# Order of the phi(k) loads on GpSimd and of the first w_down sums in a fused forward and backward kernel

## The chip, the cores and the metric

The kernel runs on one core of a Trainium2 chip. The metric is the device time of one execution in microseconds (us). Before the change it is 802.19 us, the median of 3 runs (800.33 to 802.31).

## The reference

A block of linear attention and a SwiGLU block, both behind a layer norm, forward and backward, with 2048 tokens, model width 640, 32 heads of 20, and an inner width of 1728. Inputs and outputs are bfloat16.

```python
phi = lambda t: where(t > 0, t + 1, exp(t)) + 1e-6
q, k, v = split(layernorm(x) @ wqkv)            # 32 heads
kv = einsum("hsd,hse->hde", phi(k), v);  z = phi(k).sum(over s)
o  = (phi(q) @ kv) / (phi(q) @ z + 1e-6)        # per head
h  = x + o @ wo
g, u = silu(layernorm(h) @ w_gate), layernorm(h) @ w_up
out = h + (g * u) @ w_down
# outputs: out, and the gradients of x, wqkv, wo, w_gate, w_up, w_down for a given grad_out
```

Here m = g * u, dm is its gradient, and dk, dq, dwqkv and so on are gradients. Two things of it matter below: the gradient of k needs phi(k) again late in the kernel, and `(g * u) @ w_down` is computed last of all.

## The kernel before, in words

The 2048 tokens are 16 tiles of 128 (`ST`), the width 640 is 5 blocks of 128 (`DT`), and the inner width is 4 groups of 448, 448, 448 and 384 (`GW`). TensorE (PE) multiplies into PSUM, of which a ring of 4 tiles of two banks is used. VectorE (DVE) and ScalarE (ACT) read them out. DMAs are issued from the queues of SyncE (SP), GpSimd (POOL) and ACT; each queue issues in order, so an issue that waits holds back the ones behind it. What is needed again much later is stored in scratch tensors in device memory: phi(k) in `scr_pk`, m in `scr_m`, the transposed gradients of gate and up in `scr_dT`, h in `scr_h1`.

The kernel is written with a scheduler. Inside `with tc.manual_schedule(engines={...})` the named engines keep the order of the program; the other engines' instructions are placed by the scheduler, which may put one far ahead of the place where it is written, if its operands and buffers allow it. `pool_store` (L162) issues a DMA from POOL through `keep_in_program_order`, so that it is not placed ahead; `pool_load` (L159) and a plain `nc.gpsimd.dma_start` do not.

The stages, in order, with their place in the profiled span of 803.4 us:

1. Layer norm, q, k and phi, kv, attention, and h (to about 160 us).
2. For each of the 4 groups of the inner width: gate and up, SwiGLU and its gradient (L731 to L772), and then the three weight gradients (`dw_group`, L627 to L706). The gradients of gate and up go through a transposing DMA into a `stg` tile (tag `stg`, 3 buffers) and from there to `scr_dT`. In `dw_group`, the blocks of the gradient of w_down and one row block of the others are plain products over 16 tiles (`dw`, L797 to L812); the other four row blocks are done with 7 products in place of 8, on sums and differences that DVE makes (`tt`, L642; `prod`, L646). Results are copied to `dwev` tiles of the ring `f` (6 buffers, shared with `s1` and with the SwiGLU stage) and stored from POOL (L652, L810). The end of `dw_group` in group 3 is: product with T4, `ev = fw("dwev")` filled from `pc` and `u3` by DVE, then the last product into `pc` (`ps_wc`), which has to wait until DVE has read `pc`. Group 3 ends at about 444 us.
3. The gradient of h through gate and up (`ps_dhn`, with `cols` tiles of two token tiles loaded from `scr_dT`: 0 and 1 from ACT's queue, the rest from POOL's), the gradient through wo (`ps_dp`), and dq, per token tile; to about 600 us.
4. The gradient of k and of x. Step t of the loop over 16 + 3 steps makes dk of tile t from `ps_dk` and phi(k) (`load_pk` loads tile t + 2, L933; `pkr` uses the `stg` buffers too; DVE reads it at L1037 and L1043) and dx of tile t - 3 (`ps_dxn`, then `ln_bwd`), which POOL stores (L1077). Blocks of dwqk (`dwqk_steps`, L981 to L993) stand between. SP and DVE keep program order, POOL does not.
5. The last stage, from about 730 us: out = h + m @ w_down, two token tiles a pair. Pairs 0 to 6 are done with 7 products per pair in place of 8: DVE makes T1 to T5 from w_down once and four sums S1 to S4 of m for each pair (`osum(p, i)` makes S(i+1) of pair p). PE takes `step_a` (two products of which DVE reads both, L1157 to L1163), `step_b` (S1 and T1), `step_c` (S2 and T2, into a bank that `step_a` used), `step_d` (S3, T3), `step_e` (T4, T5) and `step_f` (S4). Steps d to f of a pair run inside the next pair's turn. The last two token tiles are plain products (`tail`). Between them stand small blocks: dW_o in 6 blocks (`dwo`), dW_v in 5 (`dwv`), and what is left of dwqk (`fill`). PE and ACT keep program order here, DVE, SP and POOL are scheduled.

The change touches `load_pk` (L931 to L933), the list `small_q` (L1135) and the order of the last stage (L1202 to L1290).

Of the kernel before, what the change touches and what calls it, by code (L numbers as in the profile page):

```python
# [20 lines left out]
def kernel(  # L21
# [8 lines left out]
    nc = tc.nc  # L30
# [4 lines left out]
    DT = D // P  # L35
# [26 lines left out]
    def mm(name):  # L62

        return psum.tile([P, 2, 512], FP32, name=name, tag="mm")

    def row(ps):
        return ps[:, :, :320]

    def half(ap):
        return ap.rearrange("p (c n) -> p c n", c=2)  # L70
# [3 lines left out]
    def wk(name, w=D, pool=0):  # L74
        return wpools[pool].tile([P, w], BF16, name=name, tag="w", padded_shape=[P, D])

    def dram_tm(name, W):
        t = dram.tile([S, W], BF16, name=name)
        return t, t.rearrange("(t p) w -> p t w", p=P)

    scr_xnT = dram.tile([ST, P, DT, P], BF16, name="scr_xnT")
    scr_pk, scr_pk_v = dram_tm("scr_pk", D)
# [31 lines left out]
    HG = len(OH)  # L114
# [47 lines left out]
    def pool_store(out, in_):  # L162
        tc.keep_in_program_order(nc.gpsimd.dma_start(out=out, in_=in_))
# [452 lines left out]
    with tc.manual_schedule(engines={EngineType.SP}):  # L616
# [105 lines left out]
        for g in range(4):  # L722
# [4 lines left out]
            for t in range(0, ST, 2):  # L727
# [11 lines left out]
                tt = t % 8  # L739
# [183 lines left out]
    with tc.manual_schedule(engines={EngineType.SP, EngineType.DVE}):  # L923
# [5 lines left out]
        pkrs = {}  # L929

        def load_pk(t):  # L931
            pkrs[t] = small.tile([P, D], BF16, name="pkr", tag="stg", bufs=3, padded_shape=[P, 7 * P])
            nc.gpsimd.dma_start(out=pkrs[t][:], in_=scr_pk_v[:, t, :])  # L933

        load_pk(0)
        load_pk(1)
        def tr_cols(dst, src, c):
# [141 lines left out]
        def dwo(j):  # L1079
            h0, h1 = HC[j]  # L1080
            ev = wk("dwo", pool=j % 2)
            ps = mm("ps_dwo")
            for ci, (n0, n1) in enumerate(NCH):
                nc.tensor.matmul(ps[:, ci, :320], lhsT=KV[:, j, :], rhs=G[:, j, n0:n1], start=True, stop=True)
            nc.scalar.copy(out=half(ev[:]), in_=row(ps))
            nc.gpsimd.dma_start(out=out_3[OH[j] + h0:OH[j] + h1, :], in_=ev[h0:h1, :])
# [10 lines left out]
        def load_h1(t):  # L1097
            h1rs[t] = wk("h1r", pool=t % 2)
            nc.gpsimd.dma_start(out=h1rs[t][:], in_=scr_h1_v[:, t, :])
# [6 lines left out]
        B21, B22 = wd[:, HK:2 * HK, 0:320], wd[:, HK:2 * HK, 320:D]  # L1106
        T1, T2, T3, T4 = (ot[:, i * HK * 320:(i + 1) * HK * 320].rearrange("p (k n) -> p k n", k=HK) for i in range(4))
        T5 = ot[:, 4 * HK * 320:4 * HK * 320 + D].rearrange("p (k n) -> p k n", k=2)
# [5 lines left out]
        def os_v(p, i):  # L1114
            o = (4 * (p % 2) + i) * HK * P
            return os[:, o:o + HK * P].rearrange("p (k c) -> p k c", c=P)

        def mblk(p, r, k):
            t = 2 * p + r
            return mTs[t // 4][:, t % 4, k * HK:(k + 1) * HK, :]  # L1120

        def tt(out, in0, in1, op=ALU.subtract):
            nc.vector.tensor_tensor(out=out, in0=in0, in1=in1, op=op)

        def osum(p, i):

            if p < NP:
                S1, S2, S3, S4 = (os_v(p, k) for k in range(4))
                a11, a12, a21, a22 = mblk(p, 0, 0), mblk(p, 0, 1), mblk(p, 1, 0), mblk(p, 1, 1)
                (lambda: tt(S1, a21, a22, ALU.add), lambda: tt(S2, S1, a11), lambda: tt(S3, a11, a21),  # L1130
                 lambda: tt(S4, a12, S2))[i]()

        pa = {}
        pcc = None
        small_q = [(dwv, i) for i in range(DT)]  # L1135

        def prod(out, lhs, rhs, start, stop):
            for k in range(HK):
                nc.tensor.matmul(out, lhsT=lhs[:, k, :], rhs=rhs[:, k, :], start=(start and k == 0),  # L1139
                                 stop=(stop and k == HK - 1), skip_group_check=not start)  # L1140
# [8 lines left out]
        BL = (wd[:, 12:14, 0:320], wd[:, 12:14, 320:D])  # L1149

        def h1v(t, ci):
            return h1rs[t][:, 320 * ci:320 * ci + 320]

        def bank(p):
            return pa[p][:, 0, :320], pa[p][:, 1, :320], pcc[:, p % 2, :320]
# [13 lines left out]
        def step_c(p):  # L1169
            A = bank(p)[0]  # L1170
            prod(A, os_v(p, 1), T2, False, True)
            tt(u2h[p % 2], A, h1v(2 * p, 1), ALU.add)

        def step_d(p):
            A = bank(p)[0]
            left(A, 2 * p + 1, BL[1], 1, which=(1, 0))
            prod(A, os_v(p, 2), T3, False, True)
            tt(u3h, A, h1v(2 * p + 1, 1), ALU.add)
# [24 lines left out]
        with tc.manual_schedule(engines={EngineType.PE, EngineType.Activation}):  # L1203
            for t in range(4):
                load_h1(t)
            for t in (5, 6):
                load_mT(t)
            for j in range(2):
                tr_cols(Y[:, j, :], scr_Yt, OH[j])
            tt(T1, B12, B11)  # L1210
            osum(0, 0)
            tt(T2, B22, T1)
            osum(0, 1)
            tt(T3, B22, B12)
            osum(0, 2)
            tt(T4, B21, T2)
            tt(T5, BL[0], BL[1])
            osum(0, 3)
            fill = dwqk_steps(1, 3)
            for j in range(4):  # L1220
                next(fill)
                dwo(j)
            fill = dwqk_steps(1, 4)
            next(fill)
            dwo(4)
            pcc = mm("ps_oc")

            for p in range(NP):
                v = p - 1
                load_h1(2 * p + 4) if 2 * p + 4 < ST else None  # L1230
                load_h1(2 * p + 5) if 2 * p + 5 < ST else None
                for t in (2 * p + 7, 2 * p + 8):
                    if t < ST:
                        load_mT(t)
                for j in range(2 * p + 2, min(2 * p + 4, HG)):
                    tr_cols(Y[:, j, :], scr_Yt, OH[j])
                step_a(p)
                if v < 0:
                    next(fill)
                    osum(p + 1, 0)  # L1240
                    step_b(p)
                    step_c(p)
                    next(fill)
                    osum(p + 1, 2)
                    next(fill)
                    osum(p + 1, 1)
                    dwo(5)
                    osum(p + 1, 3)
                    continue
                step_d(v)  # L1250
                step_b(p)
                c22(v)
                osum(p + 1, 0)
                step_c(p)
                step_e(v)
                osum(p + 1, 2)
                step_f(v)
                osum(p + 1, 1)
                osum(p + 1, 3)
                if p >= 3:  # L1260
                    f, i = small_q.pop(0)
                    f(i)

            pso = {}

            def tail(u, n0, n1, out):
                for j in range(FT - 1):
                    nc.tensor.matmul(out, lhsT=mTs[u // 4][:, u % 4, j, :], rhs=wd[:, j, n0:n1],
                                     start=(u == ST - 2 and j == 0), stop=(u == ST - 1 and j == FT - 2))

            v = NP - 1
            p14 = mm("ps_o")
            tail(ST - 2, 0, 320, p14[:, 0, :320])
            step_d(v)
            tail(ST - 2, 320, D, p14[:, 1, :320])
            c22(v)
            step_e(v)
            step_f(v)
            p15 = [mm("ps_o") for _ in range(2)]
            o15 = [p15[ci % 2][:, ci // 2, :n1 - n0] for ci, (n0, n1) in enumerate(CH15)]  # L1280
            parts = [(ST - 2, n0, n1, p14[:, ci, :320]) for ci, (n0, n1) in enumerate(NCH)]
            parts += [(ST - 1, n0, n1, o15[ci]) for ci, (n0, n1) in enumerate(CH15)]
            for n, (u, n0, n1, out) in enumerate(parts):
                r = slice(64 * (n % 2), 64 * (n % 2) + 64)
                nc.tensor.matmul(out, lhsT=mTs[u // 4][r, u % 4, FT - 1, :], rhs=wd[r, FT - 1, n0:n1],
                                 start=(u == ST - 1), stop=(u == ST - 2))
            tt(half(h1rs[ST - 2][:]), row(p14), half(h1rs[ST - 2][:]), ALU.add)
            o_store(ST - 2)
            for f, i in small_q:
                f(i)  # L1290
            h1r = h1rs.pop(ST - 1)
            for ci, (n0, n1) in enumerate(CH15):
                tail(ST - 1, n0, n1, o15[ci])
                tt(h1r[:, n0:n1], o15[ci], h1r[:, n0:n1], ALU.add)
                (nc.sync, nc.scalar, nc.sync)[ci].dma_start(out=o0_v[:, ST - 1, n0:n1], in_=h1r[:, n0:n1])
# [30 lines left out]
```

## Time and profile before

| what | value |
|---|---|
| median of 3 runs | 802.19 us (800.33 to 802.31) |
| the profiled execution's own time | 805.1 us |
| its span, first to last instruction | 803.4 us |
| mean granted clock of PE in it | 0.996 of full speed |
| PE busy | 792.6 us, 99% |
| DVE, ACT, POOL busy | 566.8, 287.8, 172.6 us |
| DMA, mean over the span | 199 GB/s |

The profile is of one execution, in microseconds from the first instruction. A row of a timeline has a start, a length, the engine, the line, the operation, what is written and read, and how many instructions were merged; in brackets stands how long the engine had been idle and what released it. A view of waits has the engine and line that waited, what it waited for, the total, how often, and the longest. The rows of "stretches" have the stretch, its length, the busy time and count of PE, of its weight loads (PEld), of DVE, ACT and POOL, then the granted clock, the DMA share and GB/s. Matmuls are pipelined and their ends are modelled, so that the start of the next one says more than the end of a row.

### The profile page before, as it was taken

To read this page: it belongs to the slowest core of one execution; us is meant where nothing else is said; L and a number is where in the kernel's file an instruction comes from. 1 tells how busy PE (TensorE), PEld (TensorE's weight loads), DVE (VectorE), ACT (ScalarE), POOL (GpSimd) and SP (SyncE) were. 2 spreads that over 40 slices of the span, in tenths; PEclk is the share of its full clock that TensorE was granted. 3 is DMA by queue.
4 is the path that set the end of the run, shared out by engine and by line. 5 is a ranking of instruction groups with operands and counts; after the bars stand their busy time and mean duration, and the time that the engine had idled before them with its cause. 6 is when DMAs were issued, how large, how long until landed. Compare 5 with 4: busy or idle time off the path is not lost.

```text
span 803.4 us, 13640 instructions
## 1 busy us (share of the span) xinstructions
PE 792.6 (99%) x5315; PEld 506.5 (63%) x5315; DVE 566.8 (71%) x1015; ACT 287.8 (36%) x414; POOL 172.6 (21%) x305
## 2 busy tenths in 40 slices
PE   9999999999999999999997999999999999999998
PEld 7676566555555555555664677777777777776665
DVE  7979988894496658844954158999897366535673
ACT  7963532750382146303811123223313133323010
POOL 4600047311201110112133101111221121113320
PEclk9999999999999999999998999999999999999999
DMA  9899999999589967992897647877499869999992
GB/s 257 169 242 314 183 232 253 255 287 228 129 187 242 214 158 197 220 217 63 193 231 156 253 119 204 222 200 166 117 245 175 157 133 155 182 233 264 244 196 81
DMA packets 286706, 160.11 MB, mean 199 GB/s; under 512 B 241565, under 2 KB 275486, under 8 KB 286641
## 3 DMA queue, kind: packets, MB, share of 16 engines
q1 hardware_dynamic: 268912, 99.56, 61.5%
q0 software_dynamic: 14832, 54.36, 22.0%
q10 hardware_dynamic: 2896, 5.33, 2.2%
q8 instruction: 41, 0.67, 0.4%
q14 instruction: 25, 0.20, 0.1%
HBM read 47.68 MB, written 53.66 MB: 126 GB/s over the span
## 4 chain that ended last, share of the span: by engine, by line
PE 87%; DVE 4%; DMA 4%; issue 2%; SPq 1%; POOL 0%; ACT 0%; DVEq 0%; POOLq 0%; ACTq 0%
PE ps_dhn L108 15%; PE ps_dxn L1069 8%; PE ps_dw L806 8%; PE ps_wa L646 6%; PE pu L736 6%; PE pg L731 6%; PE ps_dm L417 5%; PE ps_dwqk L986 5%; PE ps_kq L305 4%; PE ps_oa L1139 3%; PE ps_wc L646 3%; PE ps_dp L108 3%; PE ps_y L508 3%; PE ps_gt L861 3%; PE ps_dk L108 3%; PE ps_a L571 3%
## 5 line engine op out<-in xcount | busy, mean ns | idle before, releaser
L108 PE MATMUL ps_dhn<-wgT,cols 128*128 128x320 bf16 x864 | 119.5, 299 | 0.0
L108 PEld LDWEIGHTS <-cols 128*128 128x128 bf16 x864 | 84.6, 98 | 33.0 <-issue 0.2
L146 DVE CUSTOM_DVE_ANT_0 lb_a<-lb_dy,hn 128x640 bf16<-128x640 bf16 x32 | 26.4, 825 | 59.0 <-ACT lb_dy L144 59.0
L736 PE MATMUL pu<-wgu,hnT 128*128 128x448 bf16 (+1 forms) x320 | 63.6, 346 | 0.0
L731 PE MATMUL pg<-wgu,hnT 128*128 128x448 bf16 (+1 forms) x320 | 63.6, 346 | 0.0
L806 PE MATMUL ps_dw<-m_s,dh 128*128 128x448 bf16 (+1 forms) x320 | 60.4, 346 | 0.0
L1069 PEld LDWEIGHTS <-ring 128*128 128x128 bf16 x480 | 47.0, 98 | 18.2
L1069 PE MATMUL ps_dxn<-wqkvT,ring 128*128 128x320 bf16 x320 | 51.3, 299 | 0.0
L736 PEld LDWEIGHTS <-hnT 128*128 128x128 bf16 x320 | 31.3, 98 | 27.1
L806 PEld LDWEIGHTS <-dh 128*128 128x128 bf16 x320 | 31.3, 98 | 27.1
L731 PEld LDWEIGHTS <-hnT 128*128 128x128 bf16 x320 | 31.3, 98 | 27.0
L417 PEld LDWEIGHTS <-dh2T 128*128 128x128 bf16 x320 | 31.0, 98 | 25.1
L417 PE MATMUL ps_dm<-wdT,dh2T 128*128 128x448 bf16 (+1 forms) x240 | 46.5, 344 | 0.0
L144 ACT ACTIVATE lb_dy<-ps_dhn,rstd 128x640 bf16<-128x640 f32 x16 | 12.7, 793 | 93.8 <-PE ps_dhn L108 93.8
L305 PE MATMUL ps_kq<-wqk,xnT 128*128 128x320 bf16 x320 | 44.9, 299 | 0.4 <-DMA xnT<-xn 0.4
L646 PEld LDWEIGHTS <-S 128*128 128x128 bf16 x256 | 25.7, 101 | 27.8 <-issue 7.1
L752 ACT ACTIVATE dd<-pg 128x896 bf16<-128x896 f32 (+1 forms) x32 | 28.5, 890 | 40.4 <-PE pg L731 38.0
L305 PEld LDWEIGHTS <-xnT 128*128 128x128 bf16 x320 | 30.9, 98 | 12.9 <-DMA xnT<-xn 0.8
L986 PEld LDWEIGHTS <-hn 128*128 128x128 bf16 x320 | 31.0, 98 | 12.0
L772 POOL DMA_DIRECT2D scr_m<-m_s x16 | 12.1, 756 | 122.6 <-DVE m_s L764 122.6
L642 DVE TENSOR_TENSOR dd<-dd 128x3584 bf16<-128x3584 bf16 (+1 forms) x12 | 23.1, 1953 | 21.2 <-PE ps_wa L646 21.2
L150 ACT ACTIVATE lb_a<-hn,lb_k 128x640 bf16<-128x640 bf16 x32 | 29.5, 920 | 21.7 <-DVE lb_k L149 18.8
(210 smaller groups left out, 1528.0 us busy)
## 6 DMA issues: line engine op xcount, KB each, us to landing
scr_dT<-stg SPq DMA_DIRECT2D x48, 224.0 KB, 2.6
cols<-scr_dT POOLq DMA_DIRECT2D x6, 1728.0 KB, 8.3
scr_m<-m_s POOLq DMA_DIRECT2D x12, 448.0 KB, 4.8
cols<-scr_dT ACTq DMA_DIRECT2D x2, 1728.0 KB, 12.0
scr_dT<-stg SPq DMA_DIRECT2D x16, 192.0 KB, 2.3
scr_pq<-pqa SPq DMA_DIRECT2D x4, 640.0 KB, 4.7
scr_xnT<-xnT SPq DMA_DIRECT2D x4, 640.0 KB, 5.2
scr_pk<-pk SPq DMA_DIRECT2D x4, 640.0 KB, 4.5
```

The lines of the kernel that those rows point to most:

```text
L108: nc.tensor.matmul(ps[:, ci, :320], lhsT=lhs(k), rhs=rhs(k, *NCH[ci]), start=(start and k == 0), stop=(stop and k == n - 1))
L146: nc.vector.tensor_tensor_reduce(out=a[:], in0=dy[:], in1=xhat, scale=1.0, scalar=0.0, op0=ALU.mult, op1=ALU.add, accum_out=sums[:, 1:2])
L150: nc.scalar.activation(out=a[:], in_=xhat, func=ACT.Identity, scale=k[:, 1:2], bias=k[:, 0:1])
L305: nc.tensor.matmul(ps[:, ci, :320], lhsT=xnT[:, t, k, :], rhs=wqk[:, k, w0 + n0:w0 + n1], start=(k == 0), stop=(k == DT - 1))
L417: nc.tensor.matmul(ps[:, c, :w], lhsT=dh2T[:, kt, (t + c) * P:(t + c + 1) * P], rhs=wdT[:, kt, o:o + w], start=(kt == 0), stop=(kt == DT - 1))
L646: nc.tensor.matmul(out, lhsT=lhs[:, t, :], rhs=rhs[:, t, :], start=(first and t == 0), stop=(t == 7), skip_group_check=not first)
L731: nc.tensor.matmul(pg[:, c, :w], lhsT=hnT[:, kt, (t + c) * P:(t + c + 1) * P], rhs=wg[:, kt, 0:w], start=(kt == 0), stop=(kt == DT - 1))
L736: nc.tensor.matmul(pu[:, c, :w], lhsT=hnT[:, kt, (t + c) * P:(t + c + 1) * P], rhs=wg[:, kt, w:2 * w], start=(kt == 0), stop=(kt == DT - 1))
L752: sig = nc.scalar.activation(out=dg, in_=pg[:, :, :w], func=ACT.Sigmoid)
L806: nc.tensor.matmul(ps[:, c, :w], lhsT=lhs(t), rhs=rhs(t), start=(t == 0), stop=(t == ST - 1))
L986: nc.tensor.matmul(ps[:, ci, :320], lhsT=xn_r[:, t, i * P:(i + 1) * P], rhs=dq[t // 8][:, t % 8, n0:n1] if which == 0 else dk[:, t, n0:n1] ...
L1069: nc.tensor.matmul(ps[:, ci, :320], lhsT=lhs[:, i, :], rhs=rhs[:, i, n0:n1], start=(k == 0 and i == 0), stop=(k == 2 and i == DT - 1))
```

## The change

Three things are changed, and no instruction is added or removed.

- `load_pk` issues through `pool_store`, so POOL keeps it in program order.
- In the last stage, T4, T5 and S4 of pair 0 (`osum(0, 3)`) are written after `step_a(0)`; S1 and S2 of pair 1 are written after `step_c(0)`, and T5, S4 of pair 0, S3 and S4 of pair 1 at the end of pair 0's turn.
- `dwo(5)` leaves pair 0's turn and becomes the first of `small_q`; one block is taken from it after every pair but 0 and 2 (before: from pair 3 on). The last `dwv` moves from before the last tail to behind the first block of the first tail.

```diff
         def load_pk(t):
             pkrs[t] = small.tile([P, D], BF16, name="pkr", tag="stg", bufs=3, padded_shape=[P, 7 * P])
-            nc.gpsimd.dma_start(out=pkrs[t][:], in_=scr_pk_v[:, t, :])
+            pool_store(pkrs[t][:], scr_pk_v[:, t, :])
...
-        small_q = [(dwv, i) for i in range(DT)]
+        small_q = [(dwo, HG - 1)] + [(dwv, i) for i in range(DT)]
...
             osum(0, 2)
-            tt(T4, B21, T2)
-            tt(T5, BL[0], BL[1])
-            osum(0, 3)
             fill = dwqk_steps(1, 3)
...
                 step_a(p)
                 if v < 0:
+                    tt(T4, B21, T2)
                     next(fill)
-                    osum(p + 1, 0)
                     step_b(p)
                     step_c(p)
+                    osum(p + 1, 0)
+                    osum(p + 1, 1)
                     next(fill)
-                    osum(p + 1, 2)
                     next(fill)
-                    osum(p + 1, 1)
-                    dwo(5)
-                    osum(p + 1, 3)
+                    tt(T5, BL[0], BL[1])
+                    for k, i in ((0, 3), (1, 2), (1, 3)):
+                        osum(p + k, i)
                     continue
...
-                if p >= 3:
+                if p != 2:
                     f, i = small_q.pop(0)
                     f(i)
...
             tail(ST - 2, 0, 320, p14[:, 0, :320])
+            for f, i in small_q:
+                f(i)
             step_d(v)
...
             o_store(ST - 2)
-            for f, i in small_q:
-                f(i)
             h1r = h1rs.pop(ST - 1)
```

With this, the built kernels differ in the order of the instructions as follows. POOL: before, loads 0, 1 and 2 of phi(k) stand between the first two and the next two stores of group 3's `dw` blocks; after, loads 0 and 1 stand behind the last load of x in stage 3 and the others in the step where they are written. DVE: in the last stage the two reads of `step_a(0)` stand ahead of T4, T5 and S4 of pair 0. PE: the two matmuls of `dwo(5)` and the seven of the last `dwv` stand at their new places.

## The prediction

> **What bounds the kernel now.** I read the page first, parts 1 and 2: which engine is full, and at which clock.
>
> ```profile
> PE 792.6 (99%) x5315; PEld 506.5 (63%) x5315; DVE 566.8 (71%) x1015; ACT 287.8 (36%) x414; POOL 172.6 (21%) x305
> ...
> PEclk9999999999999999999998999999999999999999
> ```
>
> TensorE (PE) is busy for 792.6 of 803.4 us. No step of this change removes a matmul, so it can only win idle PE time, 10.8 us in all, and matmuls that ran at a lower clock: slice 22 of 40 (422 to 442 us, the digit 8) is the only one under 9. Next, the waits of PE:
>
> ```profile
> PE ps_wc L646 <- DVE dwev L642: 4.4, 1, 4.4
> ...
> PE ps_oa L1139 <- DVE h1r L1123: 0.7, 1, 0.7
> PE ps_oa L1139 <- ACT dwqk L991: 0.6, 1, 0.6
> ...
> PE ps_dwv L127 <- DVE h1r L1123: 0.2, 1, 0.2
> ```
>
> These four are in code that the change touches, 5.9 us together; the others (1.1, 0.5, 0.4) are at the start. For the large one, the timeline of all engines:
>
> ```profile
> 411.31 0.80 ACT L808 CAST dwev<-ps_dw 128x768 bf16<-128x768 f32 x1 [9.12 <-PE ps_dw L806]
> ...
> 430.72 0.54 POOL L933 DMA_DIRECT2D pkr<-scr_pk  x1 [19.20 <-DMA scr_dT<-stg]
> ...
> 431.91 2.76 PE L646 MATMUL ps_wa<-m_s,hn 128*128 128x384 bf16 x16
> ...
> 434.75 0.54 POOL L933 DMA_DIRECT2D pkr<-scr_pk  x1 [1.74 <-DMA scr_dT<-stg]
> 435.29 1.08 POOL L810 DMA_DIRECT2D out_dram<-dwev  x2
> ...
> 438.10 0.96 DVE L642 TENSOR_TENSOR dwev<-ps_wc,m_s 128x768 bf16<-128x768 f32 x1 [7.37 <-DMA out_dram<-dwev]
> 439.11 5.18 PE L646 MATMUL ps_wc<-dd,S 128*128 128x384 bf16 x16 [4.44 <-DVE dwev L642]
> ...
> 444.13 6.14 PE L108 MATMUL ps_dhn<-wgT,cols 128*128 128x320 bf16 x44
> ```
>
> Three loads of phi(k), which the program writes much later, stand in POOL's queue inside group 3 of the weight gradients. They take `stg` buffers, so they wait for the stores of the last transposed tiles (until 434.1). Behind them stand two stores of a `dwev` buffer that ScalarE had filled by 412.11. They go out at 435.29 and land at 437.98. The next `dwev` of the ring needs that buffer, so VectorE waits 7.37 us and PE 4.44. The clock pays again, in the stretches before and after:
>
> ```profile
> 439.10:444.10 5.00, 4.99 (x16) 2.31 (x16) 0.00 (x0) 0.86 (x2) 2.13 (x4) 0.50 0.82 255
> 444.10:449.10 5.00, 5.00 (x38) 3.60 (x37) 0.96 (x1) 0.00 (x0) 2.36 (x4) 1.00 1.02 396
> ```
>
> The last columns but two are the granted clock: 0.50 for the 16 matmuls after the wait, then 1.00.
>
> **Part 1: loads of phi(k) in program order.** In the changed instruction order they are gone from group 3; loads 0 and 1 follow the last load of x, load t+2 stands in step t. The price of the old place is read from starts. Blocks of 32 matmuls of this shape start at 400.71, 405.91 and 411.11: 5.20 per 32, 2.60 per 16. The block of 431.91 is therefore over at 434.51, and without a wait the last block takes 2.60 more: ps_dhn starts at 437.11 and not at 444.13. That is **7.02 us**: 4.6 of waiting and 2.4 of half clock.
>
> [...] This trace had 5.0 us at 0.50. [...]
>
> What is late next here? (a) The freed stores. They can go out at 412.2, but in the built kernel a POOL transfer also waits for the one issued eight earlier, here a padding store of L163 (the second was issued at 406.94; these land 4.1 to 9.8 us after issue), so the second store goes at 416.7 at the latest. The trace has no such store in this stretch. The nearest rows for its landing: stores of L810 take 1.9 to 13.1 us, the store of `stg` issued at 409.81 beside the load of `cols` took 14.67. I take 13.1, the nearest in time: 429.8; with 14.67, 431.4. VectorE can use the buffer from 432.59, when ScalarE's copy of `u3` ends (432.11 + 0.48), and finishes at 433.6, 0.9 before PE asks. So by every row the term is 7.02, and it can't be more, since PE has no gap left; each us of landing beyond some 17 costs one. (b) `cols` 1 is loaded from ScalarE's queue behind a copy that moves from 439.15 to 434.9: issue about 435.4, landing 9.4 to 14.5 (the two loads of that queue), so 449.9 at worst. It is needed two ps_dhn steps (7.33 each in the chain) after 437.11, at 451.8. Covered by 1.9; before by 5. A later landing by x stalls PE by x - 1.9. (c) `cols` 2, now first to wait for the stores of `stg`, is needed after 466.
>
> GpSimd's issues keep 0.75 us (L772, 752 to 759 ns) while VectorE is busy 3.97 of 4.00 us. [...]
>
> In their new place the loads lie in the dk/dxn loop (one step each 5.44 us). Two of them before the xnT_r loads push those back by 1.07 (583.64 to 584.7, needed at 621.5). Load 2 goes behind the third dwqk store, at 622.7, and lands 2.5 to 6.4 us later, 629.1 at worst; VectorE wants it at 626.03, but its next operation waits for PE until 630.13. Loads 4 and 5 go behind dwqk stores at 630.3 and 636.0; they are read at 643.88 and 649.27. From load 6 on each stands behind dx(t-6): issue 644.8 against a read at 654.72, 9.9 us for a landing of 6.4 at most. Cost 0; bounds 0 and, as a rival, below.
>
> **Part 2: the first pair of w_down.** PE's timeline:
>
> ```profile
> 740.16 0.98 PE L1139 MATMUL ps_oc<-ot,os 128*128 128x320 bf16 x6
> 741.86 0.97 PE L1139 MATMUL ps_oa<-ot,os 128*128 128x320 bf16 x6 [0.72 <-DVE h1r L1123]
> 742.67 2.34 PE L986 MATMUL ps_dwqk<-dk,hn 128*128 128x320 bf16 x16
> 744.85 0.43 PE L1084 MATMUL ps_dwo<-mats 128*128 128x320 bf16 x2
> 745.84 1.79 PE L1139 MATMUL ps_oa<-wd,mT 128*128 128x320 bf16 x12 [0.55 <-ACT dwqk L991]
> ```
>
> A 320-column matmul takes 0.136 (739.07 to 740.16 for 8). Six from 740.16 end at 740.98; the next start is 741.86: **0.88** for the wait on step_a's two reads. VectorE has T4 (1.15), T5 (0.48) and S4 (0.55) ahead of them; now they follow S3, which ends at 738.95, and PE's `left` (739.14), and end at about 740.2. T4 to S4(1), 0.55 each after T4, then end near 745.7, before the next reads can start (746.0). Nothing of PE wants one earlier.
>
> With dwo(5) moved, its PSUM tile is not taken between; the next step_a gets that of dwo(4), copied by 737.86, and no longer waits for the dwqk copy. dwo(5) ends at 744.85 + 0.27 = 745.12, step_a starts at 745.84: **0.72**. dwo(5) itself (0.27 of PE, a copy of 0.70, an issue of 0.54) comes back after pair 1, where the dwv blocks of pairs 3 to 6 show no wait. Its store stands before the load of h1 tile 11, two pairs ahead of its use.
>
> The last dwv took the tile that VectorE freed at 796.47; moved up behind the first tail block it takes one copied at 789.57 before a start at 790.5, and its store leaves SP's queue ahead of three others. **0.15**; its 0.3 of matmuls is only moved. Less cover: SP transposes mT without a pause from 718 to 768, on full DMA engines. The tightest tile is 11: issue 759.15, landing 4.5 to 10.5, 769.7 at worst; VectorE's read moves from 771.45 to 769.85.
>
> **Sum.** 7.02 + 0.88 + 0.72 + 0.15 = 8.77. The profiled execution took 805.1, its span 803.4 and 1.7 around it; less 8.8, 796.3. The median of the runs, 802.19, is 2.9 below it; a wait that hangs on DMA landings may be shorter there by as much. I carry the difference over: 802.19 - 8.77 = **793.4**.
>
> **Rivals.**
> 1. Another wait takes the place in part: `cols` 1, or the freed stores, late. For: DMA is full from 400 to 424, and the cover of `cols` 1 falls to 1.9. Against: all rows end inside it. A stall of 3 us leaves a gain of 5.8 or, with the clock halved again, about 4: 796.4 to 798.2.
> 2. The large wait does not go: another load is hoisted or the store waits otherwise. Only 1.75 remains: 800.4. Against: the new order shows none there.
> 3. Slower: phi(k) arrives late in the loop. The load now stands behind dx, so it has 9.9 us from issue to read. From there each us over it costs VectorE one in each of some 10 steps, and PE after its PSUM tiles are full. A landing of 12 costs 21: 802.2 - 8.8 + 21 = 814. For: POOL transfers of up to 13.1 us exist (410, beside `cols`). Against: 6.4 at most in this loop. It decides for slower from about 10.8.
>
> **How the numbers follow.** Forecast 0.80 (own range 791.5 to 796), rival 1 0.11, rival 2 0.04, rival 3 0.05. The range reaches down by the 2 us that two runs of before differ by, up over the shorter wait (796.3) and into rival 1: 791.3 to 797.5. A measurement tells 0.3%, 2.4 us, from no change. Faster: forecast and rival 1, 0.91; same: rival 2, 0.04; slower 0.05.
>
> **What would show it.** In the changed profile: no wait of ps_wc; out_dram stores of L810 near 412 to 417; ps_dhn some 7 us earlier, at clock 1.00; the second PE wait gone, step_c right behind step_b; no wait on the dwqk copy; pkr reads without idle before them. A wait on `cols` at the third ps_dhn step is rival 1; idle before L1037 is rival 3. I am wrong if the stores of group 3 land after 433.6, or if the clock fell for another reason than the gap.

## The result and the profile after

The changed kernel takes 796.55 us (median of 6 runs, 796.16 to 798.27), the kernel before 801.35 in the same comparison (6 runs, 800.08 to 802.31): a ratio of 0.9945, 95% interval 0.993 to 0.996, 4.8 us less. The forecast was 793.4 with a range of 791.3 to 797.5: direction and range held, the gain was 4.8 and not 8.8. The time lies above the forecast's own range (791.5 to 796) and inside the one given for rival 1 (796.4 to 798.2), though the stall of rival 1 did not occur. The profiled execution of the changed kernel took 796.25 with a span of 794.5; that of before took 805.1 with 803.4. So between the two *profiles* lie 8.9 us, nearly what was forecast for them, and between the *medians* only 4.8. Where the other four went is the question of the experiments.

Page of the changed kernel, parts 1 and 2:

```profile
PE 790.2 (99%) x5315; PEld 506.5 (64%) x5315; DVE 566.9 (71%) x1015; ACT 288.1 (36%) x414; POOL 172.7 (22%) x305
...
PEclk9999999999999999999999999999999999999999
```

The digit 8 is gone, and PE is busy 2.4 us less for the same 5315 matmuls: the half clock of the profile before. The waits of PE, all that is left of them:

```profile
PE ps_warm L341 <- DVE ones L244: 1.1, 1, 1.1
PE ps_kq L305 <- DMA wqk<-in_A_wqkv_dram: 0.2, 1, 0.2
```

The timeline of all engines in group 3:

```profile
412.82 0.80 ACT L808 CAST dwev<-ps_dw 128x768 bf16<-128x768 f32 x1 [10.67 <-issue]
...
413.92 1.07 POOL L810 DMA_DIRECT2D out_dram<-dwev  x2 [2.42 <-ACT dwev L808]
...
432.58 0.96 DVE L642 TENSOR_TENSOR dwev<-ps_wc,m_s 128x768 bf16<-128x768 f32 x1 [1.89 <-ACT m_s L689]
...
434.47 2.76 PE L646 MATMUL ps_wc<-dd,S 128*128 128x384 bf16 x16
...
437.07 18.09 PE L108 MATMUL ps_dhn<-wgT,cols 128*128 128x320 bf16 x132
```

The stores follow ScalarE's copy, VectorE is released by the copy of `u3` (L689) and no longer by a DMA, the last block starts where the one before it ends, and ps_dhn starts at 437.07; 437.11 was forecast. Its first 132 matmuls, which reach past the start of the third step, run without a gap, so `cols` 1 was in time. PE's timeline in the last stage:

```profile
729.91 1.79 PE L1139 MATMUL ps_oa<-wd,mT 128*128 128x320 bf16 x12
...
733.11 0.98 PE L1139 MATMUL ps_oc<-ot,os 128*128 128x320 bf16 x6
733.92 0.98 PE L1139 MATMUL ps_oa<-ot,os 128*128 128x320 bf16 x6
734.74 2.34 PE L986 MATMUL ps_dwqk<-dk,hn 128*128 128x320 bf16 x16
736.91 1.79 PE L1139 MATMUL ps_oa<-wd,mT 128*128 128x320 bf16 x12
...
787.93 3.74 PE L1266 MATMUL ps_o<-wd,mT 128*128 128x320 bf16 x39
```

step_c follows step_b, and step_a of pair 1 follows the dwqk block, both without a wait. The first and the last row stand in the profile before as

```profile
736.97 1.79 PE L1139 MATMUL ps_oa<-wd,mT 128*128 128x320 bf16 x12
...
796.81 3.72 PE L1268 MATMUL ps_o<-wd,mT 128*128 128x320 bf16 x39
```

From the start of step_a(0) to the start of the last tail it is 59.84 us before (736.97 to 796.81) and 58.02 after (729.91 to 787.93): 1.82.

### The profile page after: what moved, and what is told of

It is laid out like the page before. It is cut to its first block, busy times and chain, and to the rows that moved or that the text cites. A ratio compares the mean times of both kernels' runs of the same rounds, so it can differ in the third digit from the quotient of the medians.

```text
span 794.5 us, 13629 instructions
## 1 busy us (share of the span) xinstructions
PE 790.2 (99%) x5315; PEld 506.5 (64%) x5315; DVE 566.9 (71%) x1015; ACT 288.1 (36%) x414; POOL 172.7 (22%) x305
## 4 chain that ended last, share of the span: by engine, by line
PE 97%; DMA 1%; DVE 1%; POOL 0%; issue 0%; SPq 0%; DVEq 0%
PE ps_dhn L108 15%; PE ps_dw L806 10%; PE ps_dxn L1069 8%; PE pu L736 7%; PE ps_wa L646 7%; PE pg L731 7%; PE ps_dwqk L986 5%; PE ps_dm L417 5%; PE ps_kq L305 4%; PE ps_oa L1139 4%; PE ps_wc L646 3%; PE ps_gt L861 3%; PE ps_dp L108 3%; PE ps_dk L108 3%; PE ps_y L508 3%; PE ps_a L571 3%
```

## The experiments

All times below stand beside runs of the kernel before on the same chip: 19 (median 802.22), 26 (801.91) and 11 (803.00) in the three groups of runs. In these 56 runs the mean granted clock over the span is given too: 30 had 1.0, with a median of 800.9 us, and 26 had less (0.993 to 0.998), with a median of 803.0.

**Theory A:** the wait in group 3 hangs on DMA landings and has another length in each execution, and the clock falls behind it in some; the profile of before caught a long one. **Rival B:** it is 4.4 us always, and the changed kernel loses something elsewhere. **Rival C:** the difference between that profile and the median lies in other stages.

### before_look1, before_look2, before_look3: the kernel before, unchanged

> The kernel before, unchanged, one more profile. The forecast of 8.8 us was the difference between two profiled executions (span 803.4 and 794.5, 8.9 apart), the medians differ by 4.8. Theory A: the profiled execution of before was caught with a longer wait in group 3 of the weight gradients, and other executions wait less there; this one should have a span of 798 to 801, the idle time before the last ps_wc block below 4 us, and the rest of the timeline equal to within 0.5 us. Rival B: the wait in group 3 is 4.4 us in every execution and the changed kernel loses something elsewhere in its ordinary runs; then this one has a span near 803.4 and the same 4.4. Rival C: the 2.9 us lie elsewhere, scattered; then the wait is 4.4, and the span shorter in other stages.

> The kernel before, unchanged, a second profile, as a second sample: theory A expects a wait of another length than in the first two, and the span to follow it one for one, with a step of up to 2.4 us where the clock falls to a half for the last block; rivals B and C expect 4.4 us again.

> The kernel before, unchanged, a third look. So far the wait of PE in group 3 was 4.44, 3.67 and 3.05 us in three profiles of it, with the clock at a half behind it in the first two. Theory A: again a wait of 2.5 to 4.5 us, and a start of ps_dhn that is 3.2 to 7.0 us later than without it. If the wait is under 1 us, part 1 of the change is worth less still on the median, and the rest of the 4.8 has another source.

PE's timeline, the last block of group 3 and the start of ps_dhn, in looks 1, 2 and 3:

```profile
438.55 5.28 PE L646 MATMUL ps_wc<-dd,S 128*128 128x384 bf16 x16 [3.67 <-DVE dwev L642]
443.62 3.60 PE L108 MATMUL ps_dhn<-wgT,cols 128*128 128x320 bf16 x23
```

```profile
438.44 2.76 PE L646 MATMUL ps_wc<-dd,S 128*128 128x384 bf16 x16 [3.05 <-DVE dwev L642]
441.04 6.14 PE L108 MATMUL ps_dhn<-wgT,cols 128*128 128x320 bf16 x44
```

```profile
437.75 2.76 PE L646 MATMUL ps_wc<-dd,S 128*128 128x384 bf16 x16 [2.38 <-DVE dwev L642]
440.35 4.92 PE L108 MATMUL ps_dhn<-wgT,cols 128*128 128x320 bf16 x35
```

The block takes 5.28 us at the half clock and 2.76 at the full one. Worked out as in the prediction, by the start of ps_dhn against the start of the block with T4 plus 5.20:

| profile | own time | wait of ps_wc | clock in the last block | ps_dhn later by |
|---|---|---|---|---|
| before | 805.1 | 4.44 | 0.50 | 7.02 |
| before_look1 | 804.92 | 3.67 | 0.50 | 6.30 |
| wd_only (below) | 800.85 | 2.58 | 1.00, then 0.50 | 4.42 |
| before_look2 | 802.02 | 3.05 | 1.00 | 3.21 |
| before_look3 | 802.14 | 2.38 | 1.00 | 2.54 |

Theory A holds: 2.4 to 4.4 us of waiting, 2.5 to 7.0 us of delay. In all five profiles the last block starts 8.25 to 8.39 us after the first of the three loads leaves POOL (430.72, 430.27, 429.03, 430.19 and 429.38, in the order of the table): so the landing for which that load waits sets when PE goes on. Look 1 missed its expected span (798 to 801; it was 803.2), while its wait, 3.67, is under 4 as expected; two of four profiles of before were long ones. Look 3, with 2.38 and 2.54, lies just under what was expected of it (2.5 to 4.5 and 3.2 to 7.0). The last stage is 59.84, 59.85 and 59.85 in the profile of before and looks 1 and 2; in look 3, with another wait of 0.6 there, 60.67. Rival B is out. Of C only a part is true: in looks 2 and 3 the T4 block itself starts 0.7 later than in the profile of before (432.63 and 432.61 against 431.91), so single executions differ by such amounts elsewhere too.

### pk_only and wd_only: each half of the change alone

pk_only is the kernel before with the first line of the change, wd_only is the change without that line.

```diff
-            nc.gpsimd.dma_start(out=pkrs[t][:], in_=scr_pk_v[:, t, :])
+            pool_store(pkrs[t][:], scr_pk_v[:, t, :])
```

> The kernel before with the loads of phi(k) kept in program order, and nothing else of the change. Theory A: no wait of ps_wc, ps_dhn starts at 437.1; the waits of 0.7, 0.6 and 0.2 in the last stage remain. The median is 4.8 - 1.75 = 3.0 us below that of before, some 798.3. If all of the 4.8 comes from the loads, 796.6. If the loads were worth 7.0 on the median, 794.3.

> The change without its first line: the sums of w_down and the blocks of dW_o and dW_v at their new places, the loads of phi(k) still placed ahead. Theory A: the wait of ps_wc remains at whatever length this execution has, the three small waits of the last stage are gone, and the median is 1.75 us below that of before, 799.6 (it must be the same in every execution, since nothing there hangs on a landing). If the last stage gains nothing on the median, 801.3.

pk_only: 798.55 (8 runs; 798.3 was expected), ratio 0.9953 (0.9932 to 0.9974), 3.7 less. No wait of ps_wc, ps_dhn starts at 437.08, and the last stage is 59.84 as before. All 8 runs have a mean clock of 1.0. wd_only: 800.12 (12 runs; 799.6 was expected), ratio 0.9984 (0.9956 to 1.0013); its time alone does not tell it from before, but in the trace its last stage is 58.02, to the hundredth that of the changed kernel. The wait of ps_wc is there, and 5 of its 12 runs have a clock under 1.0. The stretches behind that wait in wd_only (the clock is the third column from the end):

```profile
437.00:438.00 1.00, 0.59 (x4) 0.40 (x4) 0.35 (x1) 0.56 (x2) 0.62 (x2) 0.94 0.53 192
438.00:439.00 1.00, 1.00 (x5) 0.50 (x4) 0.00 (x0) 0.30 (x1) 1.00 (x3) 0.50 0.72 101
...
441.00:442.00 1.00, 1.00 (x7) 0.59 (x6) 0.12 (x1) 0.00 (x0) 0.00 (x0) 0.85 0.97 409
```

PE is at work again from 437.41, and the clock falls about half a microsecond *later*, for 3.42 us. In the profile of before it falls within the wait, while PE does nothing:

```profile
437.00:438.00 1.00, 0.00 (x0) 0.00 (x0) 0.00 (x0) 0.00 (x0) 1.00 (x3) 0.62 0.55 195
```

That is at 437.2, 2.6 us after the wait began; in look 1 it is 2.5 us (at 437.4). In both the clock stays at a half for 6.82 us, twice as long. One stretch of 3.4 us at the half clock makes a mean clock of 0.998 over the span, as here, and two make 0.996, as in the profile of before. Of the 26 runs of before under 1.0, 24 have 0.997 or 0.998 and two have 0.996 or less; so the execution that the prediction was worked out from, with 0.996, was a rare one by its clock as well.

### fill_wait: matmuls in the place of the wait

```diff
+            if g == 3:
+                pw = mm("ps_warm")
+                for _ in range(16):
+                    nc.tensor.matmul(pw[:, 0, :w], lhsT=S[0][:, 0, :], rhs=B22[:, 0, :], start=True, stop=True)
             for u in U:
                 prod(pc[:, u, :w], S[u], B22, False)
```

> The kernel before with 16 more matmuls of 384 columns (2.60 us at the full clock, into a PSUM tile that nobody reads) ahead of the last ps_wc block of group 3, where PE waits. It does more work than the reference asks for. Theory A (wait of about 3 us on the median, and a half clock in those executions in which PE stayed idle long enough): the wait shrinks to 0.4 to 1.9 us, the granted clock is 1.00 in every run, and the median falls to that of the runs of before with a mean clock of 1.0 (9 of 19, 800.4), some 1.8 below all runs of before, though PE does 2.6 us more. Rival (the clock falls for another reason than PE's idle time): about half of the runs still have a mean clock below 1.0, and the median stays at 802.

801.53 (12 runs), ratio 1.0006 (0.9989 to 1.0023). The expected 800.4 was missed. PE's timeline:

```profile
435.24 2.76 PE L703 MATMUL ps_warm<-dd,S 128*128 128x384 bf16 x16
437.84 2.76 PE L646 MATMUL ps_wc<-dd,S 128*128 128x384 bf16 x16
```

In this execution the added work fills the wait completely (VectorE ends at 437.72), with the block behind it at the full clock (2.60 us from its start at 437.84 to that of ps_dhn). But 4 of 12 runs still have a clock under 1.0, and the profiled one (809.17) shows another cause for that, a wait in the last stage that no profile had shown before (the clock is 1.00 up to 766.0 us and 0.70 from 766 to 768):

```profile
PE ps_dwv L127 <- DMA mats<-scr_Yt: 4.9, 2, 2.6
```

So the test settles little. The wait that it filled would have been some 2.4 us (from 435.40, the end of the T4 block, to 437.84), after which the clock had not fallen in look 3 either, and 4 of 12 is not clearly fewer than 26 of 56. The count over all versions tells more: of the 49 runs of versions without the wait (the changed kernel twice, pk_only, no_blocks, two_ahead, one_tile_ahead, early_y) one had a mean clock under 1.0, of the 68 with it (before and wd_only) 31. What lowered the clock in the other three runs of fill_wait is not known; they were not profiled.

### no_blocks: the sums alone, dwo(5) and the last dwv at their old places

```diff
-        small_q = [(dwo, HG - 1)] + [(dwv, i) for i in range(DT)]
+        small_q = [(dwv, i) for i in range(DT)]
...
+                    dwo(5)
                     tt(T5, BL[0], BL[1])
...
-                if p != 2:
+                if p >= 3:
```

and the loop over `small_q` behind `o_store(ST - 2)` again.

> The changed kernel with dwo(5) and the last dwv at their old places. The prediction has 0.72 for the first and 0.15 for the second: the waits on the dwqk copy (0.6) and of ps_dwv (0.2) are back, the one on step_a's reads (0.7) is not, and the median is 0.87 above that of the changed kernel, 797.4. If the sums alone had done it all, 796.55.

797.64 (11 runs), ratio 0.9954 (0.994 to 0.9968), 1.1 above the 796.55 of the changed kernel. The waits of 0.6 and 0.2 are back, that on step_a's reads is not, and the last stage is 58.96. (This profiled execution also has a wait of 1.8 us in group 3, of PE for VectorE's `dd`, in a stage that the edit does not touch; its cause was not looked for.) Against 58.02 and 59.84 this gives 0.94 to the blocks and 0.88 to the sums; 0.87 and 0.88 were forecast.

### two_ahead: loads 0 and 1 in group 3 again, the third not

```diff
-            pool_store(pkrs[t][:], scr_pk_v[:, t, :])
+            (pool_store if t else pool_load)(pkrs[t][:], scr_pk_v[:, t, :])
```

> The changed kernel with loads 0 and 1 of phi(k) back in POOL's queue inside group 3, where three stood before. They wait for earlier stores of stg tiles than the third did (430.2 and 432.0 against 434.2 in the profiles of before). Theory A: the out_dram stores go out near 432.5, land near 435.2, VectorE is done at 436.2, PE waits about 1.7 to 2.0 us at clock 1.00, and the median is 798.4 to 798.6. Rival (the third load alone, or something else in that stretch, makes the wait): either no wait and 796.6, or the same 3 us as before and 799.6.

796.97 (4 runs, 796.29 to 797.39), ratio 0.9937 (0.9916 to 0.9958). There is no wait of ps_wc in the profile, and the median is 0.4 above the changed kernel: the 798.4 of theory A was missed, the rival's 796.6 was near. POOL's timeline:

```profile
427.63 0.54 POOL L160 DMA_DIRECT2D pkr<-scr_pk  x1 [15.80 <-DMA scr_dT<-stg]
429.39 0.54 POOL L163 DMA_DIRECT2D pkr<-scr_pk  x1 [1.22 <-issue]
429.93 1.08 POOL L810 DMA_DIRECT2D out_dram<-dwev  x2
```

The stores at 429.9 are early enough for VectorE's 432.9. But only part of this is due to the missing third load. In the six profiles with three loads (fill_wait included) the third leaves 2.1 to 2.3 us after the second. The rest is this execution's own: its first load left at 427.63, 1.4 to 3.1 us earlier than in those six. With their landings, two loads would still leave an estimated 0.2 to 2.2 us of waiting (the waits of the table less 2.2). Four runs show that two loads cost little on the median, not that they cost nothing in every execution.

### one_tile_ahead and no_tile_ahead: the loads of phi(k) later in the loop

```diff
-                if t + 2 < ST:
-                    load_pk(t + 2)
+                if 1 < t + 1 < ST:
+                    load_pk(t + 1)
```

and, in no_tile_ahead, `if t > 1: load_pk(t)`.

> The changed kernel with load t + 1 in place of t + 2 written in step t of the dk/dxn loop. Rival 3 of the prediction gave a load 9.9 us from issue to read; here it has one step less, 4.5 us, against landings of 2.6 to 6.4 with a middle of 3.7. The prediction's rule: VectorE waits ahead of L1037 in the few steps with a landing over 4.5, by up to 2 us; PE has its PSUM tiles as cover, so 796.6 to 798. If the cover is smaller than reckoned, every step loses and the median is over 800.

> The changed kernel with load t (in place of t + 2) written in step t of the dk/dxn loop, so that nothing is loaded ahead. The load is issued behind dx(t-4) about 0.8 us after VectorE wants it, and lands after 3.7: rival 3 of the prediction, forced. By its rule (each us over the cover costs VectorE one in each step, and PE once its PSUM tiles are full) the excess is about 4.5 us in some 11 to 13 steps: 796.6 + 50 to 58 = 847 to 855. By the chain of VectorE in a step (0.25 + 3.7 for the load, 0.32 + 0.85 + 0.49 for dk, some 3.2 for the layer norm's gradient: 8.8 against PE's 5.44) it is 3.4 in 13 steps: 841. If loads need no lead at all, 797.

one_tile_ahead: 796.94 (8 runs; 796.6 to 798 was expected), ratio 0.9946 (0.9927 to 0.9965), 0.4 from the changed kernel's own median. VectorE waits for phi(k) twice, 3.3 us together, and PE not at all. The spare time of the new place was real. no_tile_ahead: 836.74 (2 runs), ratio 1.0415 (1.0363 to 1.0467). Its VectorE timeline, two steps, and the largest of its waits of PE:

```profile
651.00 0.33 DVE L1037 TENSOR_SCALAR pkr<-pkr 128x640 bf16<-128x640 bf16 x1 [4.43 <-DMA pkr<-scr_pk]
...
659.38 0.33 DVE L1037 TENSOR_SCALAR pkr<-pkr 128x640 bf16<-128x640 bf16 x1 [3.84 <-DMA pkr<-scr_pk]
```

```profile
PE ps_dxn L1069 <- DVE tk L1041: 20.3, 9, 3.4
```

This step takes 8.4 us (651.00 to 659.38), at the full clock; the 11 steps to 737.69 from 641.97 take 8.7 on average, instead of 5.44. From the first to the last read of phi(k) it is 124.6 us against 84.3 in the changed kernel, 40.3 more, and the median is 40.2 higher. The clock falls here too, behind PE's waits: the 5 matmuls from 668.98, behind one of 2.90 us, take 1.25 us, those from 660.49 take 0.84. It is 0.986 over the span of 834.9 us, which makes some 23 us at a half. The two steps before that fall take 8.4 and 8.5 us (651.00 to 659.38 and to 667.87), near the average, so the loads and VectorE set the step. VectorE waits for phi(k) 61.4 us in all, and the total grows by 40.2; that the rest was spare time of VectorE is worked out, not shown. The estimate by its chain (8.8 a step, 841) was near; the prediction's own rule, one for one, gave 847 to 855.

### after_again and early_y: Y out of the last stage

The wait of ps_dwv on Y showed up in the profiled execution of one_tile_ahead too (801.15, where the median was 796.94):

```profile
760.38 0.23 PE L127 MATMUL ps_dwv<-stg,mats 128*128 128x120 bf16 x1 [1.15 <-DMA mats<-scr_Yt]
761.89 0.22 PE L127 MATMUL ps_dwv<-stg,mats 128*128 128x40 bf16 x1 [1.28 <-DMA mats<-scr_Yt]
```

early_y issues the six transposes of Y in steps 2 to 7 of the dk/dxn loop:

```diff
+            if 2 <= t < 2 + HG:
+                tr_cols(Y[:, t - 2, :], scr_Yt, OH[t - 2])
             if 8 <= t < 8 + HG:
                 tr_cols(G[:, t - 8, :], scr_GT, OH[t - 8])
```

> The changed kernel, unchanged, once more on the chip of the next one: 796.55, with now and then a run some 2 to 5 us longer, in which PE waits at the first dwv for the last transposes of Y (seen in two other profiles: 2.4 and 4.9 us).

> The changed kernel with the six transposes of Y moved out of the last stage into steps 2 to 7 of the dk/dxn loop, where SP has about 1.5 us of each 5.44 free. In the last stage SP issues mT and Y without a pause, and in two profiles the first dwv waited for Y 4 and 5. Expected: no wait of ps_dwv, the mT transposes end some 9 us earlier, no run over 799, the median at 796.3 to 796.6, the same as the changed kernel within 0.3 us. Rival (the transposes only move their delay into the loop): waits of ps_dxn on ring tiles, and 798 or more.

after_again: 796.37 (6 runs, 796.02 to 797.0), ratio 0.9914 (0.9886 to 0.9941), 6.6 under the 803.00 of before in this group; the changed kernel is the steady one of the two (796.02 to 798.27 in 12 runs), so the gain depends on which runs of before it is held against. early_y: 796.6 (6 runs, 795.92 to 797.87), ratio 0.9917 (0.9887 to 0.9948). Both as expected on the median: no wait in the loop, none of ps_dwv, and no gain. SP now issues its 13 mT transposes in one row,

```profile
712.72 44.43 SPq L1028 DMA_TRANSPOSE mT<-scr_m  x13
```

done at 757.2, where in the changed kernel the same 13 end at 765.8, ahead of the first dwv store, as much as was expected. Whether it keeps off the rare late Y cannot be told: in 6 runs of after_again that did not occur either. No version tried beats the changed kernel.

## Why the prediction was right in its steps and wrong in its size

- **Part 1, the mechanism: right.** The three hoisted loads held POOL, POOL the stores, the stores VectorE, VectorE PE (in the profile of before the third load leaves at 434.75, the stores at 435.29, VectorE starts at 438.10 and PE at 439.11). pk_only removes exactly this wait; two_ahead shows that without the third load little of the wait is left on the median. In the profiles the term is 444.13 - 437.07 = 7.06; 7.02 was forecast.
- **Part 1, the size on the median: wrong, and this is the term that failed.** The term was worked out from one execution and carried over whole ("I carry the difference over: 802.19 - 8.77 = 793.4"). That execution (805.1) was above 51 of the 56 runs of before that were measured later. Over five profiles the term is 2.5 to 7.0, in pk_only 3.7 on the median, in the first comparison 4.8 - 1.8 = 3.0, in the group of after_again 6.6 - 1.8 = 4.8. The text saw the sign ("may be shorter there by as much", 796.3) and put it only into the range; 796.3 was the better forecast, and the profiled execution's own forecast, 796.3, was met by 796.25. That the median fell inside the stated range is owed to its upper part, which was there for the shorter wait and for rival 1.
- **The clock: right as a cost of the wait, not as a constant.** Behind the wait it cost 444.13 - 439.11 - 2.60 = 2.42 in the profile of before, 2.47 in look 1, 1.67 in wd_only, 0 in looks 2 and 3. The prediction's row had 5.0 us at 0.50; with the part inside the wait it was 6.82. The half clock lasted 3.42 us in wd_only and 6.82 in before and look 1. It fell with a wait of 2.58 us in one execution (wd_only) and not with one of 3.05 in another (look 2). Rival 1's lower gain, about 4, takes some 1.8 us off for a clock halved behind a stall of 3 us; that was the author's estimate, and the runs showed the costs above in its place, 1.67 to 2.47 or none.
- **Part 2: right.** 0.88 for the sums and 0.87 for the blocks were forecast, 0.88 and 0.94 are in the traces. The last stage is 59.84, 59.85, 59.85 and 59.84 in four profiles without this part (before, looks 1 and 2, pk_only) and 58.02 in all five that have it and no late Y (the changed kernel twice, wd_only, two_ahead, early_y).
- **The covers.** The freed stores go out at 413.9 and not 412.2, because ScalarE's copy starts 1.5 us later than before in this execution (412.4 in after_again); it does not matter. `cols` 1 is in time (rival 1 did not occur). Load 2 of phi(k) costs VectorE 0.4, within the 3.1 that was hidden, and the loads in the loop land within 5.7 us (6.4 was the bound). Rival 3 needs the lead of two tiles to be gone: with one tile of lead nothing is lost, with none 40 us. Its price of one for one was too high: 61.4 us of VectorE's waiting cost 40.2.
- **The cover that was named wrongly.** SP's queue in the last stage is tight, as the prediction said, but not at mT tile 11: Y 4 and 5, which stand behind mT in the same queue and are wanted by the first dwv, were late in three executions (0.6, 2.4 and 4.9 us), one of them of the kernel before.

What stays open: how the wait and the clock divide in the runs that were not profiled. The clock over the span counts every cause, and in the profiles of fill_wait and one_tile_ahead a low one (0.996 and 0.997) came with the waits for Y. At a mean clock of 1.0 the kernel before still ranges from 799.35 to 804.53, more than the waits seen in group 3 explain; what else varies was not followed. Why the three loads' buffers come free at different times was not followed either.

## What to carry to other kernels

The stall here ends with a DMA landing, and it was 2.38 to 4.44 us in five profiles, so that one profile is one draw of it: for such a stall, compare the profiled execution's own time with the median first, and forecast the median with the shorter stall. A load that the scheduler places early need not be free even if it waits for nobody's result: look at what stands behind it in its queue. Here three early loads cost 2.5 to 7.0 us, and two some 0.4 on the median of four runs. The waits here that hang on engines alone came out to the tenth (1.75 forecast, 1.82 measured).

## What the runs showed of the hardware

- The clock of PE fell to 0.50 with waits of 4.44, 3.67 and 2.58 us and not with 3.05 or 2.38; in the first two it fell 2.6 and 2.5 us after the wait began, in wd_only half a microsecond after PE had resumed. It stayed at 0.50 for 3.42 us in wd_only and 3.4 in one_tile_ahead (0.80, 0.50 and 0.85 in the three stretches of 2 us from 760), and for 6.82 us in before and look 1; in fill_wait it was an estimated 6.8, from the 0.70 of 766 to 768 and the starts of the matmuls behind (768.57 to 774.00). The profile of before has no other stretch at 0.50, that of the changed kernel only the last 0.8 us of its span. It came back 3.9 us (wd_only), 4.95 (before) and 5.7 (look 1) after PE's restart.
- Of the runs of the kernel before 26 of 56 had a mean clock under 1.0, of the changed kernel none of 12, of pk_only none of 8.
